# Linear attention feeding a two-layer MLP on one core: one group's loads queued behind an output store, and the sums of weight quarters made one at a time

## The chip, the core and the metric

The kernel runs on one core of a Trainium2 chip. The time is the device time of one execution in microseconds, and smaller is better. A core has five engines with instruction streams of their own: TensorE (PE) multiplies matrices, its weight loads (PEld) run beside the multiplications; VectorE (DVE) and ScalarE (ACT) work element by element; GpSimd (POOL) and SyncE (SP) do little here but start transfers (DMA) between DRAM and the on-chip memory SBUF. Each of the two has its own queue of transfers, in the order in which it issues them. PE writes its results to eight banks of PSUM, from where DVE and ACT take them.

## The reference

First a causal linear attention with a decay per head, over B = 4 batches, H = 8 heads, S = 768 positions and D = 64 features, in blocks of 64 positions:

```python
for b in range(S // 64):
    intra = (qb @ kb^T) * lam ** (i - j)          # within the block, j <= i
    out_b = intra @ vb + (qb * lam ** (i + 1)) @ kv_state
    kv_state = lam ** 64 * kv_state + (kb * lam ** (63 - i))^T @ vb
```

Its output, put together over the heads, is x with 3072 rows (batch, position) and 512 columns. The rest is

```python
h = x @ w_in            # 3072 x 512 times 512 x 2048
g = h - tanh(h)
out = g @ w_out         # 3072 x 2048 times 2048 x 512
```

All of it in 32-bit floating point.

## The kernel before

**Groups.** The 768 positions are cut into NG = 6 groups `g` of 128, and a group holds those positions of all four batches: 512 rows of x. The kernel does the attention of a group in blocks of 128 positions (`att_transpose`, `att_scores`, `att_out`, `att_state`), then the first product (`up`), the tanh, and the second product (`down`). Counted from one, the "second group" of the title's change is `g` = 1 and the "fourth" is `g` = 3.

**Fewer multiplications.** Group 0 is done plainly (`up_plain`, `down_plain`). Groups 1 to 5 use a scheme of Strassen's kind: both matrices of a product are cut into four quarters, and seven products of sums of quarters, numbered `n` = 1 to 7 (`FACT`), give the four quarters C11, C12, C21 and C22 of the result. In `up(g, u, n)` the 2048 hidden columns are worked in NU = 4 parts `u`. Products land in PSUM banks y, z and w; ACT copies them out or takes the tanh (L423, L438 to L445), DVE adds and subtracts (L424 to L455). A bank must have been emptied before PE begins the next product that goes to it: bank z, for instance, is emptied in group 1 by L446 or L451. For most `n` the second product (`down_twice`) uses the scheme a second time, so each of its seven products is cut into seven more, of a quarter of a quarter each; L675 is the matmul of these. `down` (L624) is the form that uses it once.

**The weights of the second product.** While group 0 runs, `sums_out` makes the sums of quarters of `w_out` that the scheme needs and stores them in DRAM, in the tensor `factors`. The sums for the second level, the tensor `fine`, are partly made there as well. The rest is made in the loop over the groups, during the first products of groups 1 and 2: `load_quarters(t)` loads the four quarters b11, b12, b21 and b22 of one factor (`t` = 0 to 4) back into SBUF, four loads on POOL; `factors_twice(t)` makes four differences on DVE (L572; each 128 partitions by 512 elements, in the order t1, t2, b12, t4) and stores them in `fine` by four transfers on POOL (L574). Its three own results lie in buffers with the tag `sums`, of which there are four, shared with other sums of that kind. For `t` = 0 and 2 the quarters lie in buffers of the ring described next, for `t` = 1 in four buffers of the tag `o`.

When a `factors_twice` comes is set by `turns`, a count of the `up` and `down` calls of the group ("steps"):

```python
turns, made = {1: (0, (7, 14, 21)), 2: (7 * NU, (1, 6))}, []
```

In group 1, `t` = 0 comes after step 7, `t` = 1 after step 14, `t` = 2 after step 21; in group 2, `t` = 3 after step 1 and `t` = 4 after step 6. Each makes its four differences in a row. After that of `t` = 0, `load_quarters(2)` issues the quarters of `t` = 2.

**The ring of weights.** `piece` (L576) streams the weight tiles of the second product (`wb`, 256 KB each) from `factors` and `fine` through RING = 7 buffers, in the order in which the products use them; POOL issues them. When a product takes its tile, the next one is asked for, and it starts once a buffer is free. The output stores of groups 1 to 4 (`store`, L597) are issued on POOL too, those of group 5 on SP.

**The loads of a group.** From `g` = 2 on, `load` issues all loads of a group at once on SP, when `att_transpose` of its first batch comes up. A batch has a "natural" tile of k and of v (`k_nat`, `v_nat`, L128, one transfer of 256 KB each) and "block" tiles of q and k (`q_blk`, `k_blk`, L141, 16 transfers of 16 KB each), which DVE transposes 32 by 32. There are 7 buffers for block tiles and 3 and 4 for `k_nat` and `v_nat`, so a transfer waits until an earlier batch is done with its buffer, and what stands behind it on SP waits with it. The order for groups 3 and 4 is: q and k blocks of batches 0, 1 and 2; q blocks of batch 3; natural tiles of batches 0 and 1; k blocks of batch 3; natural tiles of batches 2 and 3.

**Order.** The order of instructions on each engine is mostly that of the program, and a scheduler may move an instruction by its priorities and expected times. `tc.keep_in_program_order` pins one to its place: the differences of `factors_twice` on DVE are pinned, as are the loads of the later groups on SP.

**The main loop** (L791 to L850) does, for each `g` from 1 on: the first product with, from `u` = 2 on, pieces of the next group's attention; then `down` or `down_twice` for `n` = 2, 4, 5, 6, 7, 3 with the rest of that attention between them. C22 of group 1, the sum stored last by `store(g, 22, o)` in `down(g, 7)`, is made at L637.

Of the kernel before, what the change touches and what calls it, by code (L numbers as in the profile page):

```python
# [14 lines left out]
AL = mybir.AluOpType  # L15

BLK = 128
GB = 2
# [5 lines left out]
def kernel(  # L24
# [32 lines left out]
    nc = tc.nc  # L57
    B, H, S, D = q.shape
# [5 lines left out]
    NG = S // BLK  # L64
    HB = GRP // 2
    NU = DFF // 512
# [56 lines left out]
    def load_natural(g, b, names):  # L123
        for name, src, bufs in (("q", q, 2), ("v", v, 4), ("k", k, 3)) if (g, b) == (0, B - 1) else (
                ("q", q, 2), ("k", k, 3), ("v", v, 4)):
            if name in names:
                x = (qpool if name == "q" else io).tile([128, H, D], F32, name=f"{name}_nat", tag=name, bufs=bufs)
                op = nc.sync.dma_start(out=x, in_=src[b, :, ts(g, BLK), :].rearrange("h s d -> s h d"))  # L128
                if g >= GB:
                    tc.keep_in_program_order(op)  # L130
                raw[g, b][name] = x

    def load_blocks(g, b, names):
        for name, src in (("q", q), ("k", k)):
            if name in names:
                x = late["blk"].tile([128, NP, BLK // 32, 32], F32, name=f"{name}_blk", tag="blk")
                for p in range(NP):
                    for c in range(4):
                        blk = src[b, 2 * p + c // 2, ts(g, BLK), ts(c % 2, 32)]
                        tc.keep_in_program_order(  # L140
                            nc.sync.dma_start(out=x[ts(c, 32), p], in_=blk.rearrange("(r t) a -> t r a", t=32)))  # L141
                raw[g, b][name + "b"] = x

    def load(n):

        while at["loaded"] < min(n, len(chunks)):
            g, b = chunks[at["loaded"]]
            if g < GB:  # L150
                raw[g, b] = {}
                load_natural(g, b, "qkv")
                at["loaded"] += 1
                continue
            for b in range(B):
                raw[g, b] = {}
            nat = "kv" if g < NG - 1 else "v"

            first = (0, 1, 2) if g == GB else ()
            for b in first:  # L160
                load_natural(g, b, nat)
            for b in range(B - 1):
                load_blocks(g, b, "qk")
            load_blocks(g, 3, "q")
            for b in (0, 1):
                if b not in first:
                    load_natural(g, b, nat)
            load_blocks(g, 3, "k")
            for b in (2, 3):
                if b not in first:  # L170
                    load_natural(g, b, nat)
            at["loaded"] += B
# [9 lines left out]
    SUB = (1, 2, 6, 5, 7, 3, 4)  # L182
    GI = 2
    TWICE = (3, 5, 6, 4, 7)
    fine = dram.tile([len(TWICE), len(SUB), 128, NU, 128], F32, name="fine")
# [194 lines left out]
    def attention(g):  # L380
        pieces = [[(fn, g, bs) for fn in (att_transpose, att_scores, att_out, att_state)] for bs in ((0, 1), (2, 3))]
        pieces[1].append((att_sums, g, None))
        return pieces
# [81 lines left out]
    def inner_weights(u):  # L465
        for n in INNER:
            a11, a12, a21, a22 = (a_quarter(n, u, i, k) for i in range(2) for k in range(2))
            t = late["pool"].tile([128, 4, 128], F32, name="ws2", tag="sums", bufs=4)
            s1, s2, s4 = (t[:, x] for x in range(3))
            for dst, x, y, op in ((s1, a21, a22, AL.add), (s2, s1, a11, AL.subtract), (a21, a11, a21, AL.subtract),  # L470
                                  (s4, a12, s2, AL.subtract)):
                tc.keep_in_program_order(nc.vector.tensor_tensor(dst, x, y, op=op))
            nc.gpsimd.dma_start(out=fine_in[INNER.index(n)].rearrange("x p u c -> p u x c")[:, u], in_=t[:, 0:3])
# [73 lines left out]
    MADE = (4, 5, 6, 7, 3)  # L547
    quarters = {}

    def quarter_source(t, i, j):  # L550
        return factors[XAT[FACT[MADE[t]][1]]].rearrange("p (u m) c -> p u m c", m=2)[:, :, i, ts(j, 128)]

    def load_quarters(t):

        for i in range(2):
            for j in range(2):
                if t > 2:
                    quarters[t, i, j] = piece(2, ("quarter", t), 2 * i + j).rearrange("p m (v c) -> p (m v) c", v=2)
                    continue
                if t in (0, 2):  # L560
                    x = late["pool"].tile([128, NU, 128], F32, name="wq", tag="wb", bufs=RING)
                else:
                    x = opool.tile([128, NU, 128], F32, name="oq", tag="o")
                nc.gpsimd.dma_start(out=x, in_=quarter_source(t, i, j))
                quarters[t, i, j] = x

    def factors_twice(t):

        b11, b12, b21, b22 = (quarters.pop((t, i, j)) for i in range(2) for j in range(2))
        t1, t2, t4 = (late["pool"].tile([128, NU, 128], F32, name=f"wt{x}", tag="sums", bufs=4) for x in (1, 2, 4))  # L570
        for dst, x, y in ((t1, b12, b11), (t2, b22, t1), (b12, b22, b12), (t4, b21, t2)):
            tc.keep_in_program_order(nc.vector.tensor_tensor(dst, x, y, op=AL.subtract))  # L572
        for x, src in ((5, t1), (6, t2), (7, b12), (4, t4)):
            nc.gpsimd.dma_start(out=fine[TWICE.index(MADE[t]), SUB.index(x)], in_=src)  # L574

    def piece(g, n, x):  # L576

# [19 lines left out]
    def store(g, c, t):  # L597
        i, j = divmod(c - 11, 10)
        rows = out.rearrange("(b s) d -> s b d", b=B)[ts(g, BLK), 2 * i:2 * i + 2, ts(j, 256)]
        eng = nc.sync if g == NG - 1 else nc.gpsimd  # L600
        eng.dma_start(out=rows, in_=t.rearrange("q (m c) -> q m c", m=2))

    def otile(name):
        return opool.tile([128, 512], F32, name=name, tag="o")
# [95 lines left out]
    def every(steps):  # L700
        for _ in steps:
            pass
# [81 lines left out]
    late["pool"] = ctx.enter_context(tc.tile_pool(name="late", bufs=1))  # L784


    turns, made = {1: (0, (7, 14, 21)), 2: (7 * NU, (1, 6))}, []
    load_quarters(0)
    load_quarters(1)
    up(1, 0, 1)  # L790
    for g in range(1, NG):  # L791
        last = g == NG - 1
        p0, p1 = attention(g + 1) if not last else ([], [])
        for u in range(NU):
            for n in (2, 6, 5, 7, 1, 4, 3) if g < GI else (1, 7, 3) if u == 0 else (6, 5, 1, 7, 3) if u + 1 < NU else (
                    6, 5, 7, 1, 3):
                if n != 1:
                    up(g, u, n)
                elif u + 1 < NU:
                    up(g, u + 1, 1)  # L800
                else:
                    every(down(g, 1))
                if g in turns:
                    made.append(n)
                    step = len(made) - turns[g][0]
                    if step in turns[g][1]:
                        t = turns[g][1].index(step) + len(turns[1][1]) * (g - 1)
                        if t > 2:
                            load_quarters(t)
                        factors_twice(t)  # L810
                        if t == 0:
                            load_quarters(2)
            if g == GI - 1:
                inner_weights(u)
            if not last and u > 1:
                run(p0[u - 2:u - 1])
        sums_twice(g, 4)
        every(down(g, 2))
        run(p0[2:])
        sums_twice(g, 5)  # L820
        every(down_twice(g, 4, "z"))
        run(p1[0:1])
        sums_once(g, 21, 21, 11)
        sums_twice(g, 6)
        every(down_twice(g, 5, "w"))
        run(p1[1:2])
        if twice(g, 7):
            sums_twice(g, 7)
        every(down_twice(g, 6, "z"))
        if twice(g, 3):  # L830
            sums_twice(g, 3)
        run(p1[2:])
        every(down_twice(g, 7, "w") if twice(g, 7) else down(g, 7))
        if last:
            down_end(g)
            continue
        inner_tokens(g + 1)
        p3 = down_twice(g, 3, "z") if twice(g, 3) else down(g, 3)
        p2 = inner_steps(g + 1, 2, "yb")
        for kind, _ in in_turn(g):  # L840
            next(p3 if kind == "down" else p2)
        every(p2)
        every(p3)
        p4 = inner_steps(g + 1, 4, "yb")
        for n in (None, None, 1, None, None, 6, None, None, 5, None):
            if n is None:
                next(p4)
            else:
                up(g + 1, 0, n)
        every(p4)  # L850
# [30 lines left out]
```

## Time and profile before

| | us |
|---|---|
| median of three runs | 678.42 (677.26 to 679.59) |
| the profiled execution | 679.9 |
| span of its instructions | 678.0 |
| PE busy | 663.4 |
| DVE busy | 481.2 |
| POOL busy | 201.5 |
| ACT busy | 200.9 |

The span runs from the first instruction to the last. The stretches of it, by the profile's windows, with the clock that was granted to PE as a share of the full one and the mean busy share of the 16 DMA engines:

| stretch (us) | what runs | PE busy | clock | DMA |
|---|---|---|---|---|
| 0 to 29 | start, attention of group 0 | 21.05 of 29 | 1.00 | 0.96 |
| 29 to 226 | group 0, first product of group 1 | 197.00 of 197 | 1.00 | 0.82 |
| 226 to 240 | second product of group 1 begins | 12.04 of 14 | 0.88 | 0.97 |
| 240 to 340 | rest of group 1, first product of group 2 | 99.18 of 100 | 1.00 | 0.68 |
| 340 to 648 | groups 2 to 5 | 308.00 of 308 | 1.00 | 0.58 |
| 648 to 678 | end of group 5 | 26.11 of 30 | 1.00 | 0.66 |

A row of a timeline has the start of an instruction in us, its length in us, the engine, the line of the kernel, the operation, what it writes and reads (out<-in) with the tile sizes, and in brackets how long the engine had been idle ahead of it and what released it. "SPq" and "POOLq" are the DMA queues of SP and POOL, "x16" says that sixteen instructions are in the row. Line numbers are those of the kernel before.

### The profile page before, as it was taken

What the parts mean: (1) busy time and instruction counts of PE and PEld (TensorE: products, weight loads), DVE (VectorE), ACT (ScalarE), POOL (GpSimd) and SP (SyncE); (2) the same over time, 40 slices, a digit from 0 to 9 for tenths busy, and PEclk for the clock granted to TensorE, in tenths of its full rate; (3) what the DMA queues carried; (4) which work ended last, traced back from release to release, by engine and by line L of the source; (5) the groups of instructions that cost most, each with busy time, mean ns of one, the idle gap of its engine ahead of it and who ended that gap; (6) DMA issues with size and microseconds to landing.
All of it is one profiled execution on the core that took longest, in us unless ns stands there. A gap on an engine that the chain in (4) does not pass through costs nothing.

```text
span 678.0 us, 12935 instructions
## 1 busy us (share of the span) xinstructions
PE 663.4 (98%) x4832; PEld 577.3 (85%) x4832; DVE 481.2 (71%) x878; ACT 200.9 (30%) x398; POOL 201.5 (30%) x348
## 2 busy tenths in 40 slices
PE   6899999999999899999999999999999999999998
PEld 5788855558888899988999988899988899988897
DVE  3798758894889853299887368988358977357743
ACT  2764432423331211243112243112333122334120
POOL 0001424216444334241254300255300244400351
PEclk9999999999999999999999999999999999999999
DMA  9779979959967977576698741598840686610494
GB/s 187 216 212 230 293 217 255 297 145 258 255 180 218 267 194 191 137 198 186 162 297 251 211 95 30 150 286 244 245 85 9 154 246 203 224 44 1 119 294 161
DMA packets 162957, 129.59 MB, mean 191 GB/s; under 512 B 133904, under 2 KB 135056, under 8 KB 162896
## 3 DMA queue, kind: packets, MB, share of 16 engines
q0 software_dynamic: 29216, 97.28, 45.6%
q1 hardware_dynamic: 133536, 31.50, 23.2%
q8 instruction: 38, 0.62, 0.4%
q14 instruction: 23, 0.19, 0.1%
q10 hardware_dynamic: 144, 0.00, 0.0%
HBM read 104.34 MB, written 24.38 MB: 190 GB/s over the span
## 4 chain that ended last, share of the span: by engine, by line
PE 87%; DMA 4%; issue 3%; POOL 2%; DVE 1%; SPq 1%; ACT 0%; POOLq 0%; DVEq 0%; ACTq 0%
PE y L415 16%; PE y L675 10%; PE z L415 10%; PE h L724 8%; PE op L740 8%; PE zw L675 7%; PE y L499 4%; PE w L624 4%; PE y L624 4%; PE sp L313 3%; PE op L364 3%; PE z L499 2%; PE plain L624 2%; DMA wb<-fine 2%; POOL wb L589 2%
## 5 line engine op out<-in xcount | busy, mean ns | idle before, releaser
L589 POOL DMA_DIRECT2D wb<-fine x154 | 83.0, 539 | 126.1 <-PE y L675 53.3
L423 ACT ACTIVATE th<-g 128x512 f32<-128x512 f32 x76 | 47.5, 630 | 98.5 <-DVE g L428 31.8
L415 PE MATMUL y<-xt,w 128*128 128x256 f32 x320 | 74.0, 381 | 0.7 <-ACT g L443 0.7
L592 POOL DMA_DIRECT2D wb<-factors x52 | 28.2, 543 | 145.2 <-PE y L624 98.4
L415 PEld LDWEIGHTS y<-xt,w 128*128 128x128 f32 x320 | 59.8, 190 | 10.0 <-ACT g L443 1.1
L424 DVE TENSOR_TENSOR g<-g,th 128x512 f32<-128x512 f32 x76 | 51.8, 688 | 18.3 <-ACT th L423 17.9
L678 ACT ACTIVATE q<-y 128x128 f32<-128x128 f32 x88 | 24.4, 277 | 122.7 <-PE y L675 121.9
L740 PE MATMUL op<-wt,g 128*128 128x512 f32 x128 | 56.5, 595 | 0.0
L724 PE MATMUL h<-xt,w 128*128 128x256 f32 x256 | 56.1, 381 | 0.0
L675 PE MATMUL y<-wb,g 128*128 128x128 f32 x408 | 54.4, 278 | 0.1
L724 PEld LDWEIGHTS h<-xt,w 128*128 128x128 f32 x256 | 48.3, 190 | 7.3 <-issue 0.3
L675 PEld LDWEIGHTS y<-wb,g 128*128 128x128 f32 x408 | 49.3, 192 | 1.5 <-issue 0.7
L740 PEld LDWEIGHTS op<-wt,g 128*128 128x128 f32 x128 | 23.8, 190 | 27.7 <-issue 26.5
L317 DVE TENSOR_TENSOR ss<-sp,mask 128x512 f32<-128x512 f32 x48 | 30.9, 682 | 11.7 <-PE sp L313 11.7
L415 PE MATMUL z<-tt,ws 128*128 128x256 f32 x160 | 38.1, 381 | 0.0
L415 PE MATMUL y<-tt,ws 128*128 128x256 f32 x160 | 38.0, 379 | 0.0
L415 PE MATMUL z<-xt,ws 128*128 128x256 f32 x160 | 37.9, 380 | 0.0
L197 POOL DMA_DIRECT2D raw<-in_moe_w_out_dram x16 | 8.8, 553 | 92.2 <-DMA raw<-in_moe_w_in_dram 54.0
L675 PE MATMUL zw<-wb,g 128*128 128x128 f32 x272 | 36.0, 275 | 0.1
L624 PE MATMUL w<-wb,g 128*128 128x256 f32 x160 | 35.8, 382 | 0.0
L624 PE MATMUL y<-wb,g 128*128 128x256 f32 x160 | 35.3, 379 | 0.0
L415 PEld LDWEIGHTS z<-xt,ws 128*128 128x128 f32 x160 | 30.3, 190 | 4.3 <-ACT g L431 0.2
(169 smaller groups left out, 1299.5 us busy)
## 6 DMA issues: line engine op xcount, KB each, us to landing
wb<-fine POOLq DMA_DIRECT2D x154, 256.0 KB, 3.8
wb<-factors POOLq DMA_DIRECT2D x60, 256.0 KB, 4.1
raw<-in_moe_w_out_dram POOLq DMA_DIRECT2D x16, 512.0 KB, 5.1
v_nat<-in_v_dram SPq DMA_DIRECT2D x24, 256.0 KB, 5.3
factors<-wt POOLq DMA_DIRECT2D x8, 768.0 KB, 5.2
wb<-fine_in POOLq DMA_DIRECT2D x24, 256.0 KB, 4.1
k_nat<-in_k_dram SPq DMA_DIRECT2D x20, 256.0 KB, 5.2
raw<-in_moe_w_in_dram SPq DMA_DIRECT2D x8, 512.0 KB, 5.7
```

What stands on the lines that cost most here:

```text
L317: nc.vector.tensor_tensor(ss[:, j], sp[j], mask[:, j], op=AL.mult)
L415: nc.tensor.matmul(out=t[:, m, :], lhsT=wt[:, kt, ts(m, 128)], rhs=x[:, kt, :], start=first and m == 0 and kt == 0, stop=kt == 1, skip_gro ...
L423: nc.scalar.activation(th, src, AF.Tanh)
L424: nc.vector.tensor_tensor(dst(c), src, th, op=AL.subtract)
L499: nc.tensor.matmul(out=dst[:, ts(u, 128)], lhsT=a, rhs=b, start=x in (1, 2, 5) and u == 0, stop=True, skip_group_check=True)
L589: nc.gpsimd.dma_start(out=t.rearrange("p m c -> p (m c)"), in_=fine[TWICE.index(n_), SUB.index(x_)].rearrange("p u c -> p (u c)"))
L592: nc.gpsimd.dma_start(out=t, in_=factors[XAT[FACT[n_][1]]][:, 2 * x_:2 * x_ + 2, :])
L624: nc.tensor.matmul(out=t[:, m, :], lhsT=a[:, u, kt, ts(m, 128)], rhs=wb[:, kt, :], start=first and u == 0 and m == 0 and kt == 0, stop=u = ...
L675: nc.tensor.matmul(out=dst, lhsT=a[:, u, :], rhs=wb[:, ts(u, 128)], start=x in (1, 2) and u == 0, stop=u == NU - 1, skip_group_check=True)
L678: nc.scalar.activation(keep, dst, AF.Copy)
L724: nc.tensor.matmul(out=hm[:, m, :], lhsT=w1[u][:, i, a, ts(m, 128)], rhs=xt[0, t][:, i, :], start=m == 0 and i == 0, stop=i == KI - 1, ski ...
L740: nc.tensor.matmul(out=obank[b], lhsT=g, rhs=wt[:, 2 * a:2 * a + 2, :], start=kt == 0 and a == 0, stop=kt == KH - 1 and a == 1)
```

## The change

It has three parts.

1. `load`: for `g` = 3 alone, the natural tiles of batches 0 and 1 are now issued ahead of the blocks of batch 2. The order becomes: blocks of batches 0 and 1, natural tiles of 0 and 1, q and k blocks of batch 2, q and k blocks of batch 3, natural tiles of 2 and 3.
2. `store`: C22 of group 1 is stored on SP, no longer on POOL, and is pinned to its place in the program's order. `load` issues group 3's loads later in the program than this store, and all of them are pinned too, so on SP they stand behind the store, which waits until L637 has made C22.
3. `factors_twice` becomes a generator: one difference, its store, and a pause. The main loop calls for one at each of four successive steps. In group 1 `t` = 0 is spread over steps 5 to 8, `t` = 1 over 12 to 15 and `t` = 2 over 20 to 23; in group 2 `t` = 3 over steps 1 to 4 and `t` = 4 over 6 to 9. `load_quarters(2)` moves from step 7 to step 8. The differences and the transfers are the same, and each store follows its own difference.

```diff
@@ load
-            for b in range(B - 1):
-                load_blocks(g, b, "qk")
+            load_blocks(g, 0, "qk")
+            load_blocks(g, 1, "qk")
+            if g == GB + 1:
+                first = (0, 1)
+                for b in first:
+                    load_natural(g, b, nat)
+            load_blocks(g, 2, "qk")
             load_blocks(g, 3, "q")
@@ factors_twice
-        for dst, x, y in ((t1, b12, b11), (t2, b22, t1), (b12, b22, b12), (t4, b21, t2)):
-            tc.keep_in_program_order(nc.vector.tensor_tensor(dst, x, y, op=AL.subtract))
-        for x, src in ((5, t1), (6, t2), (7, b12), (4, t4)):
-            nc.gpsimd.dma_start(out=fine[TWICE.index(MADE[t]), SUB.index(x)], in_=src)
+        for x, dst, a, b in ((5, t1, b12, b11), (6, t2, b22, t1), (7, b12, b22, b12), (4, t4, b21, t2)):
+            tc.keep_in_program_order(nc.vector.tensor_tensor(dst, a, b, op=AL.subtract))
+            nc.gpsimd.dma_start(out=fine[TWICE.index(MADE[t]), SUB.index(x)], in_=dst)
+            yield
@@ store
-        eng = nc.sync if g == NG - 1 else nc.gpsimd
-        eng.dma_start(out=rows, in_=t.rearrange("q (m c) -> q m c", m=2))
+        gate = (g, c) == (1, 22)
+        op = (nc.sync if gate or g == NG - 1 else nc.gpsimd).dma_start(
+            out=rows, in_=t.rearrange("q (m c) -> q m c", m=2))
+        if gate:
+            tc.keep_in_program_order(op)
@@ main loop
-    turns, made = {1: (0, (7, 14, 21)), 2: (7 * NU, (1, 6))}, []
+    turns = {1: (0, ((0, 5), (1, 12), (2, 20))), 2: (7 * NU, ((3, 1), (4, 6)))}
+    made, making = [], {}
...
-                    if step in turns[g][1]:
-                        t = turns[g][1].index(step) + len(turns[1][1]) * (g - 1)
-                        if t > 2:
-                            load_quarters(t)
-                        factors_twice(t)
-                        if t == 0:
+                    for t, first in turns[g][1]:
+                        if step == first:
+                            if t > 2:
+                                load_quarters(t)
+                            making[t] = factors_twice(t)
+                        if first <= step < first + 4:
+                            next(making[t])
+                        if (t, step) == (0, first + 3):
                             load_quarters(2)
```

## The prediction

> **What bounds the kernel now.** I read the page's busy times first, then the waits, then timelines wherever TensorE (PE) starts late. The page, busy times (us, share of the span, instructions):
>
> ```profile
> PE 663.4 (98%) x4832; PEld 577.3 (85%) x4832; DVE 481.2 (71%) x878; ACT 200.9 (30%) x398; POOL 201.5 (30%) x348
> ```
>
> PE idles 678.0 - 663.4 = 14.6 us. About 8 us lie before 29 us and about 4 us at the end, both untouched. So only stalls and half-clocked matmuls in the middle can be won. The largest shows in four views put below each other: SP's timeline (start, busy us, instruction), the transfer row of the one weight tile `wb` issued at 228.10, PE's timeline, and busy times by stretch (stretch, its length, busy us of PE, PEld, DVE, ACT, POOL with the slow-down of each, granted clock, DMA share, GB/s):
>
> ```profile
> 226.44 0.39 SPq L128 DMA_DIRECT2D k_nat<-in_k_dram  x1
> 226.88 0.59 SPq L128 DMA_DIRECT2D v_nat<-in_v_dram  x1
> 227.51 13.71 SPq L141 DMA_DIRECT2D q_blk<-in_q_dram  x16
> DMA to landing us min/median/max: 7.3/7.3/7.3
> 232.55 1.16 PE L675 MATMUL zw<-wb,s 128*128 128x128 f32 x8
> 235.56 1.59 PE L675 MATMUL y<-wb,gS 128*128 128x128 f32 x8 [1.85 <-DMA wb<-fine]
> 232.66:236.07 3.41, 1.55 (x12) 1.39 (x13) 2.76 (x7) 0.54 (x2) 1.07 (x2) 1.00 1.07 320
> 236.07:239.48 3.41, 3.41 (x18) 3.41 (x17) 0.71 (x2) 0.28 (x1) 0.85 (x2) 0.50 0.86 250
> ```
>
> Groups of eight such matmuls start every 0.89 us, so the one at 235.56 was due at 233.44: a stall of about 2.1 us, on a `wb` that took 7.3 us, with 0.3 us more at 227.5. In the second stretch the clock is 0.50 for 3.41 us, which costs half of it, 1.7 us. Together 4.1 us. A second stall is one row of PE's timeline in group 2 of the loop `g` (start 301.07, due about 300.2): 0.9 us, on ACT.
>
> ```profile
> 301.07 1.13 PE L415 MATMUL y<-xt,w 128*128 128x256 f32 x4 [0.69 <-ACT g L443]
> ```
>
> [...] 1.55 of 3.41 us busy, then 0.50 for 3.41 us. [...] The rows of DVE quoted below start in the order in which the program issues them. [...] `wb` landed after 3.1 us at 224.53, after 7.3 us at 228.10 behind the natural tiles.
>
> **Part 1, sums one by one.** DVE work stays at 20 sums of 0.69 us; POOL issues the same 20 stores. What moves is when DVE meets each. For t=0 the four sums stood together after step 7 of group 1; now t1 stands right behind the L424 that ran at 165.62, t2 one L424 later, and both stand ahead of the L451 that empties PSUM bank z. The order of the changed program's DVE stream says so, and its waits: t1 needs quarters b11 and b12, t2 needs b22. These are the four `wq` loads. POOL's timeline, the issue row of the fourth (ns, then its time) and that load's time to landing:
>
> ```profile
> 164.84 2.96 POOL L564 DMA_DIRECT2D wq<-factors  x4 [3.42 <-issue]
> L564 POOL DMA_DIRECT2D wq<-factors x1: 747/747/747, 167.1 to 167.1; - x1
> DMA to landing us min/median/max: 5.9/5.9/5.9
> ```
>
> b22 lands at 167.06 + 5.87 = 172.9; b12 at 165.58 + 4.67 = 170.25. Nothing ahead of these loads changes. The timelines of DVE, ACT and PE there before:
>
> ```profile
> 165.62 0.69 DVE L424 TENSOR_TENSOR g<-g,th 128x512 f32<-128x512 f32 x1 [0.69 <-ACT th L423]
> 168.79 0.69 DVE L451 TENSOR_TENSOR g<-g,z 128x512 f32<-128x512 f32 x1 [0.35 <-PE z L415]
> 172.98 0.69 DVE L572 TENSOR_TENSOR wt<-wq 128x512 f32<-128x512 f32 x1
> 171.61 0.63 ACT L423 ACTIVATE th<-g 128x512 f32<-128x512 f32 x1 [1.42 <-DVE g L440]
> 172.24 0.60 ACT L443 ACTIVATE g<-y 128x512 f32<-128x512 f32 x1
> 172.04 1.89 PE L415 MATMUL z<-tt,ws 128*128 128x256 f32 x8
> 173.77 3.62 PE L415 MATMUL y<-xt,w 128*128 128x256 f32 x16
> ```
>
> After: t1 at 170.3, L424 at 170.95, t2 at 173.0, L451 at 173.6 to 174.3. PE's z product (due 172.04) waits for that: it starts at 174.35, 2.3 us late. Its 1.73 us end at 176.1, and the y product needs ACT's L443, which queues behind two tanh: tanh 174.4 to 175.0, DVE L424 175.05, L440 175.65 to 176.35, tanh to 177.05, L443 to 177.65. So y starts at 177.7 instead of 173.77: 3.9 us late in all. PE has no slack to give it back. The two idle stretches (2.3 and 1.6 us) make a throttled window likely. At half clock the z product's lateness hides under the second wait, so 0 to 0.9 us, and 1.7 us more if a second window trips: between 0 and 2.6, I take 1.0. Later waits on the four `sums` buffers (stores of 3 to 5 us to landing, 5 or more us ahead of their next writer) and on the ring hide.
>
> In group 2 the sums no longer stand four abreast (2.4 us of DVE, 297 to 300), and the y product that waited at 301.07 stands behind others. Walking the new order with the same rows, the z product is about 0.15 us late there: gain 0.9 - 0.15 = 0.75; bounds 0 and 0.9.
>
> **Part 2, group 3's loads behind C22.** SP gains one store (256 KB; POOL loses its 0.72 us of issue). Behind it queue 128 block loads and 8 natural ones, which began at 227.51 and now wait for L637 of group 1, about 261. What does that free? Packets of group 3's blocks moved only from about 232; until then the natural tiles of group 2 (226.44, 226.88) filled the engines, and those don't move on SP. Alone, the gate saves some 0.6 us of DMA time ahead of the late `wb` (about 800 packets of 128 B at 0.012 us over 16 engines): the stall would shrink to 1.5 us. But the 3.9 us of part 1 shift PE against SP: the natural tiles then issue at about 227 while the first `y<-wb` of down_twice starts at 227 too. That is the position of group 2 before, where blocks followed as well and PE did not stall. SP's timeline there, and the time to landing (min, median, max) of the seven `wb` loads from 336.46:
>
> ```profile
> 334.65 0.37 SPq L128 DMA_DIRECT2D k_nat<-in_k_dram  x1
> DMA to landing us min/median/max: 4.3/4.5/4.6
> ```
>
> The ring of 7 at 0.89 us bears about 5.3 us. So stall and half clock go: -4.1. Bounds: -0.6 and -4.6 (0.5 us of ripples behind it).
>
> Are the loads late? From 261, at 7.7 us per 16 blocks, q0, k0, q1, k1 are issued by 292 and land by 296; DVE transposes them from 312.6. Two natural pairs take 292 to 301 as before (their first use is at 329), q2, k2, q3 until 325, k3 until 333, landing 336 to 338; DVE transposes it at 343.4. Slack 5 us; SP is back at its old place for group 4 (335.9). Cost 0. If the cover went, each us of lateness of k3 beyond 5 would hold DVE, then PE.
>
> **Sum.** +3.9 + 1.0 - 0.75 - 4.1 = +0.05, say 0, against the profiled execution (span 678.0, whole 679.9). That run is above the median of 678.42, perhaps by a throttled window of 1.7 us; some runs may lack it, which takes from the gain, and ripples add 0.3. I take 678.2. About 0.3% (2 us) is what a measurement of this kernel can tell from no change.
>
> **Cases.**
> - Trade (45%): the above, 678.2, own range 676.4 to 680.4.
> - Slower (24%): the early wait is paid and the late stall stays, because natural tiles still meet `wb`, or both idle stretches trip windows (+3.9 + 1.7 - 1.5 - 0.5 = +3.6): 682. It decides from a landing of `wb` above 5.3 us after the shift. For it: those natural tiles still stand in the same stretch as the loads of `wb`; against: group 2's rows.
> - Faster (23%): the `wq` quarters land early enough, or the wait is short, while the gate works: -0.6 to -4.6 and -0.75 give about 675. It decides from b22 landing before 170.5. For it: DMA latencies move by a us or two; against: those loads start only after a store lands at 164.24, in both kernels.
> - Loads late (4%): k3 lands after 343; 681 and up.
> - No effect (4%): the shifted sums hit no wait and the gate frees nothing: 678.4.
>
> Chances by the bound: faster 0.26, same 0.47, slower 0.27. Range 674.8 to 681.8.
>
> **What would show it.** Right: a DVE wait on the landing of `wq` at about 171.6 to 173; PE gaps of 2.3 us before `z<-tt,ws` near 172 and 1.6 us before `y<-xt,w` near 176; half clock near 175 to 180; SP's store near 261 with `q_blk` behind it; no PE wait on `wb` from 227 to 245; no gap near 300; DVE never waiting for `q_blk` or `k_blk`. Wrong: no gap at 172 (then faster), or a PE wait on `wb` after 227 all the same (then slower).

## The result: 0.59% slower, and where it shows in the profile

The changed kernel takes 681.98 us (median of 8 runs, 681.12 to 684.85), the kernel before 678.15 us (8 runs, 677.08 to 680.09). The ratio is 1.0059 with a 95% interval of 1.0039 to 1.0080: 4.0 us slower, 2.6 to 5.4. The profiled execution took 681.97 us with a span of 679.9 us. PE's own work is what it was; it has more gaps. The page, busy times:

```profile
PE 662.5 (97%) x4832; PEld 575.9 (85%) x4832; DVE 480.4 (71%) x878; ACT 201.2 (30%) x398; POOL 200.9 (30%) x347
```

Lines have moved by the edit: L577 is the sum that was L572, L456 the addition that was L451, L420 and L684 the matmuls that were L415 and L675. First the place of the early sums, DVE's and PE's timelines of the changed kernel (start, busy us, instruction, in brackets how long the engine had been idle and what released it):

```profile
171.30 0.69 DVE L577 TENSOR_TENSOR wt<-wq 128x512 f32<-128x512 f32 x1 [4.22 <-DMA wq<-factors]
171.91 0.68 DVE L429 TENSOR_TENSOR g<-y,th 128x512 f32<-128x512 f32 x1
174.17 0.69 DVE L577 TENSOR_TENSOR wt<-wq,wt 128x512 f32<-128x512 f32 x1 [1.57 <-DMA wq<-factors]
174.78 0.68 DVE L456 TENSOR_TENSOR g<-g,z 128x512 f32<-128x512 f32 x1
175.51 1.99 PE L420 MATMUL z<-tt,ws 128*128 128x256 f32 x8 [2.53 <-DVE g L456]
178.76 3.50 PE L420 MATMUL y<-xt,w 128*128 128x256 f32 x15 [1.26 <-ACT g L448]
```

DVE twice stands and waits for a quarter that has not landed. What stood behind a waiting sum on DVE waited with it: the tanh that L429 takes was made by ACT from 167.90 to 168.50, and L429 started at 171.91, behind the first sum. L456, which empties bank z, is behind both sums. The z product should have followed the y product that began at 171.09, 1.73 us later, as before; it started at 175.51, 2.7 us late. The next product, due another 1.73 us later, waited for ACT and started at 178.76, 1.5 us late again: 4.2 us in all. (The listed length of a row, 1.89 or 1.99 us, is longer than the distance at which rows follow each other, so the brackets show less than this.) Before, PE was busy through all of this.

Second, the weight tiles of `down_twice`, in group 1 and in group 2. SP's timeline, with the four rows of PE that waited:

```profile
229.43 0.39 SPq L128 DMA_DIRECT2D k_nat<-in_k_dram  x1
238.75 1.13 PE L684 MATMUL y<-wb,gS 128*128 128x128 f32 x8 [0.15 <-DMA wb<-fine]
240.19 1.13 PE L684 MATMUL zw<-wb,gS 128*128 128x128 f32 x8 [0.31 <-ACT q L687]
263.40 0.39 SPq L607 DMA_DIRECT2D out_dram<-q  x1
341.00 0.38 SPq L128 DMA_DIRECT2D k_nat<-in_k_dram  x1
346.28 1.13 PE L684 MATMUL y<-wb,gS 128*128 128x128 f32 x8
348.00 1.13 PE L684 MATMUL zw<-wb,gS 128*128 128x128 f32 x8 [0.59 <-DMA wb<-fine]
```

At 0.89 us per group of eight, PE loses 0.9 us around 238 to 241, where before it lost 2.2 us and then a half-clocked window. But it now loses 1.1 us at 346 to 348 (from 345.13 to 348.00 are 2.87 us for two groups of 0.89), where the kernel before lost nothing:

```profile
344.93 1.06 PE L675 MATMUL y<-wb,gS 128*128 128x128 f32 x8
345.82 1.06 PE L675 MATMUL zw<-wb,gS 128*128 128x128 f32 x8
```

In the changed kernel SP had just come to the last natural tiles of group 3 (341.00). Before, these were issued at 321.94 to 335.06, ahead of the weight tiles of this stretch, the first of which was issued at 336.46. In group 2's first product there is no wait any more in the changed kernel:

```profile
302.17 1.89 PE L420 MATMUL y<-xt,w 128*128 128x256 f32 x8
```

### The profile page after: what moved, and what is told of

It reads as the page before. It is cut to its first block, busy times and chain, and to the rows that moved or that the text cites. A ratio compares the mean times of both kernels' runs of the same rounds, so it can differ in the third digit from the quotient of the medians.

```text
span 679.9 us, 12929 instructions
## 1 busy us (share of the span) xinstructions
PE 662.5 (97%) x4832; PEld 575.9 (85%) x4832; DVE 480.4 (71%) x878; ACT 201.2 (30%) x398; POOL 200.9 (30%) x347
## 4 chain that ended last, share of the span: by engine, by line
PE 66%; issue 14%; DMA 8%; POOL 5%; DVE 5%; ACT 1%; SPq 1%; POOLq 0%; DVEq 0%; ACTq 0%
PE y L420 11%; PE y L684 8%; PE z L420 7%; PE h L733 6%; PE zw L684 6%; PE op L749 5%; PE y L504 4%; POOL wb L594 3%; PE w L633 3%; PE y L633 3%; PE sp L318 3%; PE plain L633 2%; DMA raw<-in_moe_w_in_dram 2%; PE op L369 2%; PE z L504 2%
## 5 line engine op out<-in xcount | busy, mean ns | idle before, releaser
L420 PE MATMUL y<-xt,w 128*128 128x256 f32 x320 | 73.9, 381 | 1.3 <-ACT g L448 1.3
L420 PEld LDWEIGHTS y<-xt,w 128*128 128x128 f32 x320 | 59.8, 190 | 10.6 <-ACT g L448 1.7
L429 DVE TENSOR_TENSOR g<-g,th 128x512 f32<-128x512 f32 x76 | 51.9, 688 | 18.9 <-ACT th L428 18.7
L684 PE MATMUL y<-wb,g 128*128 128x128 f32 x408 | 54.5, 278 | 0.0
L684 PEld LDWEIGHTS y<-wb,g 128*128 128x128 f32 x408 | 49.3, 192 | 1.5 <-issue 0.3
L420 PE MATMUL z<-tt,ws 128*128 128x256 f32 x160 | 38.2, 382 | 2.5 <-DVE g L456 2.5
L420 PE MATMUL y<-tt,ws 128*128 128x256 f32 x160 | 37.8, 379 | 0.0
L420 PE MATMUL z<-xt,ws 128*128 128x256 f32 x160 | 37.8, 379 | 0.0
L684 PE MATMUL zw<-wb,g 128*128 128x128 f32 x272 | 36.0, 275 | 0.1
L420 PEld LDWEIGHTS z<-tt,ws 128*128 128x128 f32 x160 | 29.4, 190 | 7.7 <-DVE g L456 3.8
```

Source lines behind the costliest of these rows:

```text
L420: nc.tensor.matmul(out=t[:, m, :], lhsT=wt[:, kt, ts(m, 128)], rhs=x[:, kt, :], start=first and m == 0 and kt == 0, stop=kt == 1, skip_gro ...
L429: nc.vector.tensor_tensor(dst(c), src, th, op=AL.subtract)
L684: nc.tensor.matmul(out=dst, lhsT=a[:, u, :], rhs=wb[:, ts(u, 128)], start=x in (1, 2) and u == 0, stop=u == NU - 1, skip_group_check=True)
```

## The experiments

Each is timed beside the kernel before, apart from two second profiles. Ratios are to the kernel before; 0.1% is 0.68 us. A ratio on record is not always the quotient of the two medians (for the sums alone, 681.38 to 678.59 would be 1.0041 and not 1.0035); differences "slower" and "faster" in us below are worked out from the ratios. Line numbers of these kernels differ by a few: L675 of before is L684, L683, L677 or L686.

| kernel | ratio | 95% interval |
|---|---|---|
| changed kernel | 1.0059 | 1.0039 to 1.0080 |
| sums one by one alone | 1.0035 | 1.0021 to 1.0048 |
| gate and order of loads alone | 1.0021 | 1.0002 to 1.0039 |
| changed, sums at steps 7, 14, 21 | 1.0018 | 1.0005 to 1.0030 |
| changed, t = 0 in a row | 1.0005 | 0.9992 to 1.0018 |
| the same without gate | 0.9995 | 0.9981 to 1.0010 |
| changed, t = 0 from step 6 | 1.0016 | 1.0005 to 1.0028 |
| changed, natural tiles of three batches early | 1.0069 | 1.0049 to 1.0089 |
| before, one v tile early | 0.9976 | 0.9964 to 0.9988 |
| v tile early, t = 0 in a row, no gate | 0.9947 | 0.9928 to 0.9966 |
| the same with gate | 0.9980 | 0.9970 to 0.9991 |

### Each half of the change alone

The sums alone are the changed kernel with its gate and its order of loads undone:

```diff
-            if g == GB + 1:
+            if False:
...
-        gate = (g, c) == (1, 22)
+        gate = False
```

> Part 3 alone: the sums one by one, with the kernel before's order and place of all loads and of C22's store. My theory (the two sums of t=0 that meet their quarters too early hold DVE, and so the emptying of bank z): two gaps of PE at about 172.6 and 177.1, 4.1 us together (2.7 and 1.4), as in the changed kernel; near 300 no gap (0.95 us gained). The shift of about 4 us moves the natural tiles of the second loop group ahead of the burst of weight tiles, so the stall of 2.2 us at 232 to 236 shrinks to 1 to 1.5 us even without the gate. Time about 682, 3.5 to 4.5 us above before. Rival (the gate causes the loss): no gap at 172, and a time within 1 us of before.

Measured: 681.38 us against 678.59, 2.4 us slower (1.4 to 3.3). Both gaps are there, with no gate, and the wait near 300 is gone; the stall on weight tiles is 0.9 us at 241 to 243. So the early sums alone bring the first loss, and the late stall shrinks without the gate, because PE now runs later than SP: here the two natural tiles are issued 7.0 us ahead of the first product `y<-wb,gS` (230.89 and 237.93), in the changed kernel 5.4 us, in two profiles of the kernel before 3.3 and 0.9. The time came out below the expected 3.5 to 4.5. The profiled execution, the slowest of the 22, shows what the same wait costs when the clock is halved behind it (PE's timeline, then stretches: their length, busy us of the five engines, granted clock, DMA share and GB/s):

```profile
176.26 2.68 PE L420 MATMUL z<-tt,ws 128*128 128x256 f32 x8 [2.63 <-DVE g L456]
179.51 6.04 PE L420 MATMUL y<-xt,w 128*128 128x256 f32 x16 [0.57 <-ACT g L448]
174.01:177.43 3.42, 1.17 (x5) 1.06 (x6) 1.76 (x3) 0.63 (x1) 0.56 (x1) 1.00 1.08 305
177.43:180.84 3.41, 2.84 (x7) 1.82 (x6) 3.38 (x7) 1.11 (x2) 0.37 (x1) 0.50 0.53 143
180.84:184.25 3.41, 3.41 (x9) 2.69 (x9) 2.45 (x10) 0.60 (x1) 3.03 (x6) 0.50 0.60 142
```

A stretch with PE busy for 1.17 of 3.42 us is followed by two at half clock. The y product of `tt` that follows started at 185.39; without a wait it was due at 178.65, after 1.73 and 3.45 us of matmuls from 173.47. The loss is 6.7 us, 2.5 more than in the changed kernel's profile, near the prediction's upper end of 2.6. It happens in part of the executions: 10 of 22 had a mean granted clock of 0.998 or less. (By my working, one window of 3.41 us at a clock of 0.50 takes 0.0025 from the mean of 680 us; the first profile of the kernel before, with one, has a mean of 0.997, and this one, with two, 0.995. Where in the span such a window lay is known for the profiled executions only.)

The gate alone is the kernel before with the diff's hunks for `load` and `store`:

```diff
+            if g == GB + 1:
+                first = (0, 1)
+                for b in first:
+                    load_natural(g, b, nat)
...
+        gate = (g, c) == (1, 22)
+        op = (nc.sync if gate or g == NG - 1 else nc.gpsimd).dma_start(
```

> Parts 1 and 2 alone: C22 on SP ahead of group 3's loads, natural tiles of two batches earlier, all sums as in the kernel before. My theory: no gap at 172; the stall of PE on a weight tile at 232 to 236 shrinks from 2.2 us to about 1.5 us, because the blocks' packets no longer compete with the last of that burst; the wait near 300 stays at 0.95 us; group 3's loads land before they are needed. Time 0.3 to 1 us below before: 677.2 to 677.9. Rival (the loads behind the gate come too late): DVE waits for q_blk or k_blk between 310 and 345, PE gaps there, 681 or more.

Measured: 679.91 us, 1.4 us slower (0.1 to 2.6): neither theory's number. DVE waits for blocks only 0.4 us, at 341.99, and there is no gap at 172; the stall near 233 is 1.6 us, as expected; but a new loss came up in group 2:

```profile
338.75 0.38 SPq L128 DMA_DIRECT2D k_nat<-in_k_dram  x1
339.18 0.58 SPq L128 DMA_DIRECT2D v_nat<-in_v_dram  x1
345.85 1.13 PE L683 MATMUL y<-wb,gS 128*128 128x128 f32 x8 [0.74 <-DMA wb<-fine]
```

This is the price that the prediction had set to nothing, without the early wait beside it. The gate and the order of loads were not run apart from each other, so how the price divides between them stays open. The losses of the halves, 2.4 and 1.4 us, add up to 3.8 of the 4.0 us.

### Moving the early sums

First all of group 1's sums later, still one by one:

```diff
-    turns = {1: (0, ((0, 5), (1, 12), (2, 20))), 2: (7 * NU, ((3, 1), (4, 6)))}
+    turns = {1: (0, ((0, 7), (1, 14), (2, 21))), 2: (7 * NU, ((3, 1), (4, 6)))}
```

> The changed kernel with the first sum of t = 0, 1 and 2 at steps 7, 14 and 21 in place of 5, 12 and 20, still one by one. My theory: t1 now stands behind the row of DVE that empties bank z, when its quarters have landed; the gaps at 172 and 177 go (4.1 us), at most 0.3 us remains near 179 where t4 waits for a buffer; the gap near 300 stays away. Time about 677, 1 us below before. Rival (the four-step spread itself, with its buffers, is what costs): still 3 us or more above before, with gaps elsewhere between 172 and 200.

Measured: 679.65 us, 1.2 us above before and 2.8 below the changed kernel. The gaps at 172 and 177 are gone; the fourth sum waits 0.94 us for a buffer, and PE's row behind it, at 178.75, starts 0.4 us late, where at most 0.3 had been expected. The time expected was 2.6 us too low; this kernel still has the gate and its loss, 1.0 us at 344, and a stall of 2.1 us at 233 to 236.

Then t = 0 alone put back in a row after step 7, the rest as changed:

```diff
-                        if first <= step < first + 4:
+                        if t == 0 and step == first:
+                            every(making[t])
+                        elif t and first <= step < first + 4:
                             next(making[t])
-                        if (t, step) == (0, first + 3):
+                        if (t, step) == (0, first):
```

> The changed kernel with the four sums of t = 0 alone in a row after step 7, as in the kernel before, and t = 1 to 4 one by one as changed. My theory: the loss of 4.1 us lies in t = 0 alone, so it goes; up to 0.3 us near 185, where t = 1's second sum waits for a store of t = 0's. Time about 677.3. Rival (the early starts of t = 1 and t = 2 cost as well): gaps of 1 us or more at 184 to 200, and 679 or more.

Measured: 679.32 us, not told apart from before, 3.7 us below the changed kernel (0.54% of 678). So t = 0 is the whole of the first loss; t = 1 and 2 left no gap of 1 us between 184 and 200. Expected was 677.3; the gate's loss (0.9 us at 344) and a stall of 1.8 us near 235 are still there.

Then a dose: one step later than in the change, so that only t1 stands ahead of L456.

```diff
-    turns = {1: (0, ((0, 5), (1, 12), (2, 20))), 2: (7 * NU, ((3, 1), (4, 6)))}
+    turns = {1: (0, ((0, 6), (1, 12), (2, 20))), 2: (7 * NU, ((3, 1), (4, 6)))}
```

> The changed kernel with t = 0 at steps 6 to 9 in place of 5 to 8: now only t1 stands ahead of the row of DVE that empties bank z (L456), t2 behind it. A dose of the suspected wait. My theory: t1 can start when b12 has landed, 171.3 in the changed kernel's trace, so L456 ends at about 172.6, 1.7 us earlier than there: the gap before z<-tt,ws is 0.7 us in place of 2.7, the following y<-xt,w waits about 1.3 us, together 2.0 us in place of 4.1. Time 2 us below the changed kernel, 680 or so. Rival (the wait is for t2's landing or for buffers, whatever the step): both gaps stay within 0.5 us of the changed kernel's.

Measured: 679.85 us, 2.9 us below the changed kernel. DVE's and PE's timelines:

```profile
170.12 0.69 DVE L577 TENSOR_TENSOR wt<-wq 128x512 f32<-128x512 f32 x1 [1.83 <-DMA wq<-factors]
170.72 0.68 DVE L456 TENSOR_TENSOR g<-g,z 128x512 f32<-128x512 f32 x1
171.88 1.89 PE L420 MATMUL z<-tt,ws 128*128 128x256 f32 x8
174.71 3.72 PE L420 MATMUL y<-xt,w 128*128 128x256 f32 x16 [0.94 <-ACT g L448]
```

The quarter landed 1.2 us sooner than in the changed kernel's profile (and 0.7 us sooner than in its second one, below), though nothing ahead of it was changed. L456 then came early enough for the z product, and only the second gap remained, 1.1 us of the 4.2; 2.0 had been expected. Taking one of two sums from ahead of one instruction took 3.1 us from the gaps and 2.9 us from the time. With the two kernels above, where no sum stands ahead of L456 and the gaps are gone, this shows the wait as the cause. That the loss follows the length of the wait rests on this profile, which is of the fastest of 14 executions (677.61 us).

### The gate's price

> Part 3 alone, with t = 0 in a row as in the kernel before: no gate, no other order of loads, t = 1 to 4 one by one. My theory (the gate costs about 1 us, by the loss near 346): no loss near 346, no wait near 300 (0.95 us gained), the stall near 233 as before: 0.7 to 1.3 us below before, and 1 us below the same kernel with the gate. Rival (the gate costs nothing of its own): no difference to the kernel with the gate, 0 to 0.5 us above before.

This is the kernel with t = 0 in a row, and the gate undone as in the first experiment. Measured: 677.86 us against 678.36, a ratio of 0.9995: 0.7 us below the same kernel with the gate, by ratios whose intervals overlap. There is no loss near 346, PE busy without a break in the window there:

```profile
340.00:350.00 10.00, 10.00 (x103) 9.76 (x103) 8.32 (x15) 1.66 (x6) 4.55 (x10) 1.00 1.02 298
```

The wait near 300 is gone too, and yet little of its 0.95 us appears in the time; the stall near 233 was 2.0 us here.

To try the natural tiles as the cause, the changed kernel with one batch more of them issued early:

```diff
-                first = (0, 1)
+                first = (0, 1, 2)
```

> The changed kernel, with the natural tiles of group 3's batch 2 issued together with those of batches 0 and 1, ahead of the blocks of batch 2; only batch 3's natural tiles stay behind the last k blocks. All kernels with the gate lost about 1 us of PE at 344 to 348, where before lost none, with four natural tiles issued at 339 to 344 amid the weight tiles, and wb landings of 5.9 to 7.6 us. My theory (a new collision at the end of the late loads): with two natural tiles instead of four, wb there lands in 5.5 us or less and the loss near 346 falls to 0.4 us or less; the rest as in the changed kernel; 0.7 us better. Rival (group 4's blocks or the blocks of batch 3 cause it): the loss near 346 stays at about 1 us.

Measured: 683.57 us, a ratio of 1.0069 against the changed kernel's 1.0059 with intervals that overlap: not faster. The landings did fall at first: of the `wb` tiles issued at 341 to 344 the time to landing (min, median, max) was

```profile
DMA to landing us min/median/max: 4.1/4.2/4.3
```

against 5.0 to 6.3 us for tiles issued then in the changed kernel. But here SP came to the natural tiles of batch 3 only at 344.22, and the four `wb` tiles issued behind them, at 344.76 to 347.44, took 6.0 to 6.3 us again. So two natural tiles in place of four moved the slow landings and did not cure them. PE did not come to wait for those tiles, since it stood for another reason. What was put in front pushed the k blocks of batch 3 back, and those came too late (DVE and PE):

```profile
347.48 0.71 DVE L298 STREAM_TRANSPOSE kt<-k_blk 128x512 f32<-128x512 f32 x1 [2.79 <-DMA k_blk<-in_k_dram]
349.47 1.13 PE L684 MATMUL zw<-wb,gS 128*128 128x128 f32 x8 [2.32 <-issue]
```

PE's row waits behind that transposition, since the sum L689 whose result it reads stands two places after it on DVE and started at 348.68. So the loads behind the gate have no room: with natural tiles last they run into the weight tiles, with more of them first the blocks are late. The landings point to the natural tiles as the cause of the loss near 346. In the changed kernel the `wb` tile issued at 340.24, ahead of the first of them (341.00), landed after 4.0 us; those issued at 341.13 and 342.02 took 5.0 and 5.8. The blocks of batch 3 were still being issued while tiles landed in 4.1 to 4.3 us here, and group 4's blocks began at 346.02 in the changed kernel, when the first of its late tiles had landed. No run takes the natural tiles out of this stretch and leaves all else, so this is read from the order of events and not isolated.

### The stall near 233, and a faster kernel

The kernel before, with the natural v tile of group 2's batch 3 issued with those of batches 0 to 2, so that only the k tile comes at the bad moment:

```diff
             for b in first:
                 load_natural(g, b, nat)
+            if g == GB:
+                load_natural(g, 3, "v")
...
-                    load_natural(g, b, nat)
+                    load_natural(g, b, "k" if (g, b) == (GB, 3) else nat)
```

> The kernel before, with the natural v tile of group 2's batch 3 issued with those of batches 0 to 2; only k of batch 3 stays at 226. My theory (natural tiles of 256-byte packets hold up the weight tiles at 228): the wb issued near 228.1 lands about 1.2 us sooner, so the stall of PE near 233 to 236 falls from 2.2 us to about 1, and a half-clocked window after it becomes rare: 1 to 2 us below before. Rival (group 3's blocks, which follow at once, hold them up): they start half a us sooner, and the stall stays at 2 us or grows.

Measured: 676.98 us, 1.6 us faster (0.8 to 2.4). That half-clocked windows became rarer is not shown: 2 of 22 executions had a mean granted clock of 0.998 or less, and 4 of 43 of the kernel before that ran beside it. PE's only late row between 229 and 237, with SP's row of the k tile:

```profile
230.33 0.38 SPq L128 DMA_DIRECT2D k_nat<-in_k_dram  x1
235.74 1.13 PE L677 MATMUL y<-wb,gS 128*128 128x128 f32 x8 [0.19 <-DMA wb<-fine]
```

It started 0.36 us late (235.74 - 234.49 - 0.89), in place of 1.7 to 2.2 us. One tile of 256 KB in the wrong microsecond was most of that stall. (In the kernel before, between 230 and 232 us, SP's queue moved 1061 packets with 0.27 MB, about 254 bytes each, and POOL's 101 packets with 0.35 MB; the profile counts both on the same 16 DMA engines.) The early v tile together with t = 1 to 4 one by one and t = 0 in a row, without the gate:

> A kernel made of the two things that helped: the v tile of group 2's batch 3 loaded early, and the sums of t = 1 to 4 one by one with t = 0 in a row; no gate. My theory (independent terms): no stall near 233, no wait near 300; the gain of the early v tile (1.6 us) plus that of the spread sums in group 2 (0.95 us): 2 to 2.6 us below before. Rival (the terms overlap): no better than the early v tile alone, 1.6 us below.

Measured: 675.73 us against 678.79, a ratio of 0.9947 (0.9928 to 0.9966): 3.6 us faster than before, and the fastest kernel here. That is more than the 2 to 2.6 expected, and more than the two parts had shown (1.6 and 0.3 us); with six executions and an interval that meets that of the early v tile alone, how much the spread sums add stays open. The same with the gate and its order of loads:

> The same with the gate and its order of loads. My theory (the gate has one small use, the stall near 233, and one price, the loss near 346): with the stall already gone it has only its price, about 1 us at 344 to 348: 0.7 to 1.5 us slower than the same kernel without it. Rival (the gate costs nothing): equal to it.

Measured: 677.48 us, 2.2 us slower than without. The gate has no stall left to relieve near 233. Its profile is of the slowest of its 22 executions (679.66 us), and in it PE loses about 1.3 us at 233 to 238, where the kernel without the gate lost nothing; the gate holds transfers back there, so it does not explain this. Then comes the loss that belongs to the gate:

```profile
342.73 1.13 PE L686 MATMUL y<-wb,gS 128*128 128x128 f32 x8 [0.46 <-DMA wb<-fine]
344.62 1.13 PE L686 MATMUL zw<-wb,gS 128*128 128x128 f32 x8 [0.76 <-DMA wb<-fine]
```

Four pairs differ in the gate and its order of loads alone: before, 1.4 us; sums alone, 1.6; t = 0 in a row, 0.7; early v tile and t = 0 in a row, 2.2. The mean is 1.5 us. In two of the four pairs the intervals are clear of each other or of no change: before, and the last.

### Second profiles

> The kernel before once more, for a second profile. The first had a half-clocked window of 3.4 us after the stall near 233, and took 679.9 us with a median of 678.4. My theory: the stall of about 2 us is there in each execution, the half-clocked window is not: span 676 to 677. Rival: both are always there, and a span near 678.

Measured: 677.18 us, span 675.3. PE is at full clock all through the stretch where the first profile had a half-clocked window, and the stall is 1.7 us (two rows, due at 233.85 and 235.55):

```profile
234.66 1.13 PE L675 MATMUL zw<-wb,gS 128*128 128x128 f32 x8 [0.64 <-DVE gS L680]
236.46 1.13 PE L675 MATMUL y<-wb,gS 128*128 128x128 f32 x8 [0.67 <-DMA wb<-fine]
226.00:240.00 14.00, 12.59 (x121) 11.86 (x121) 10.94 (x23) 2.22 (x8) 6.40 (x12) 1.00 1.00 295
```

Of the 137 executions of the kernel before that were timed beside the experiments, 22 had a mean granted clock of 0.998 or less; their median was 680.9 us, that of the others 678.4. The profile that the prediction worked from was one of the minority.

> The changed kernel once more. My theory: the gaps at 172 and 177 are there again, 4.1 us within 0.3, and a loss of about 1 us near 346; the gap of 1.1 us near 44, which stands ahead of everything that was changed, is chance and may be absent. Rival: the gap near 44 belongs to the change and is there again.

Measured: 680.92 us, span 678.8. Gaps of 2.4 and 1.5 us, 3.95 together; 0.9 us at 238; about 1.1 us at 345 to 347. The first profile had a gap of 1.05 us at 44, ahead of all that was changed; here there is none, so that one was chance.

The two second profiles against each other give the balance: +3.95 at 172 to 177, -0.8 at 233 to 240, -0.95 near 300, +1.1 near 346, together +3.3. The spans differ by 3.5. The two executions were already 0.6 us apart at 170 us, ahead of all that was changed, so the balance can be trusted to about that.

## Why the prediction was wrong

**Part 1, the early wait: right.** The two sums wait for b12 and b22, L456 stands behind them, the z product waits for DVE and the y product for ACT. 3.9 us were predicted, 4.2 and 3.95 measured, and one sum less ahead of L456 moved gap and time alike. That a waiting DVE instruction holds those behind it was taken as given; the rows of L577 and L429 in the changed kernel show it, and so do L577 and L456, of which the second started at 174.78 there and at 170.72 with one sum less ahead of it. The 1.0 us for throttling (half-clocked windows) was an estimate; its measured ground was one stretch, 3.41 us at a clock of 0.50 behind the stall of 2.1 us. It stood for something that happens or does not: 0 in both profiles of the changed kernel at that place, 2.5 in the one of the sums alone. In group 2, 0.75 us were predicted as gained, and 0.95 us of wait went.

**"So stall and half clock go: -4.1": the step that failed most.** Its mechanism is partly right: the shift of PE against SP shrinks the stall, to 0.9 us with the gate and without it, while the gate without the shift left 1.6 us (gate alone), 1.8 (t = 0 in a row) and 2.1 (steps 7, 14, 21). But its size was taken from one execution. The half-clocked window is 1.7 us of the 4.1; a mean clock as low as one such window gives is on record for about a sixth of the executions of the kernel before, so it is no part of the median. And the stall does not go but shrinks, from 1.7 or 2.2 us to 0.9: the tile issued at 233.20 still took 5.4 us to land, just over the 5.3 that the ring was said to bear. The gain is 0.8 us by the two second profiles (1.3 us by the first two), in place of 4.1. The prediction did say that its profile lay above the median, "perhaps by a throttled window of 1.7 us", and then only noted that this takes from the gain; it had to take it out of the sum.

**"Are the loads late? ... Cost 0": wrong.** The estimate asked when k3 lands, and stopped there. SP's queue was later than worked out, too. The gate opened at 263.4, not 261, as PE itself was late, but by 300.49 the queue was where the working had it. Then the 16 blocks of q2, behind the natural tiles, took 14.55 us to issue where 7.7 were assumed; the prediction's own row at 227.51 has 13.71 us for 16 blocks behind natural tiles. The last blocks were issued by 340.9, not 333, and DVE came to k3 at 344.83 after 0.19 us of idling: the 5 us of slack were not there. Behind k3 stand four natural tiles and group 4's blocks, and these met the weight tiles of group 2. "SP is back at its old place for group 4 (335.9)" was in truth 346.02. The price is 1.1 us in the profiles, and 1.5 us in time for the gate and its order of loads as a whole, where -0.6 had been the least gain thought possible.

**The sum, redone** with what was measured: +4.1 - 0.95 - 0.8 + 1.1 = +3.45, against 2.6 to 5.4. What half-clocked windows add is left out of it: 5 of 8 executions of the changed kernel had a mean clock of 0.998 or less, against a sixth before.

**The cases.** "Slower" gave 682, with 24%, and is what came: the early wait paid and a late stall on `wb` left. But part of its price lies where no case had looked, in group 2, and the case counted 1.7 us for a second window that neither profile has near 175; that its number fits so well is in part luck. "Loads late" had the right queue and the wrong victim. The range ended at 681.8 and the median is 681.98: it was made from a likeliest case that credited a rare window as a gain.

## What to carry to other kernels

Before you credit a removed stall, see whether it is in the typical execution: a profile that lies above the median may hold something that most others lack. When a queue is held back, follow it to its end: price every transfer behind the gate, the last ones above all, against what they now land beside. And a sum that waits for a transfer must not stand ahead of an instruction that frees a buffer for the busiest engine; put behind that instruction, the same four sums left no gap (t = 0 in a row).

## What the runs showed of the hardware that I had not expected

Gaps of 2.3 to 2.8 us were followed by PE at half clock in one profile, and not in others. In the sums alone PE stood for 2.63 us ahead of 176.26 and for 0.57 us ahead of 179.51, by the brackets, and the granted clock was 0.50 from 177.43 to 184.25, two stretches of 3.41 us; in the 3.42 us ahead of them PE was busy for 1.17 us. Nor was the stretch idle that stands ahead of the half-clocked one in the prediction's profile: PE was busy for 1.55 of 3.41 us. The changed kernel's two profiles, and the one with natural tiles of three batches early, have gaps as long there (2.3 to 2.8 us and 1.26) with a mean granted clock of 1.0, so something besides their length decides. What that is, no run here shows.

One natural tile of 256 KB, moved out of a burst of weight tiles, was worth 1.6 us of 678. It is 0.26 of the 129.6 MB that the kernel moves; what counted was when it came.
